# Sixteen spare products on TensorE ahead of a three-stage attention kernel's first scores

## The chip, the cores and the metric

The kernel runs on one core of one Trainium2 chip, as one program. The metric is the device time of that program in microseconds (us), as the median of several runs. Engines are named as in the profile: PE (TensorE products), PEld (TensorE weight loads), DVE (VectorE), ACT (ScalarE), POOL (GpSimd), SP (SyncE, which here issues the transfers).

## The reference

Three stages follow one another, in fp32, for 2 batches, 768 positions and 512 channels (8 heads of 64).

1. Local attention with block summaries. Each query sees the keys less than 16 positions away, and one summary for each block of 32 positions (the maximum over the block's keys, the mean over its values):

```
k_sum = k.reshape(B, H, nb, block, D).max(axis=3)
v_sum = v.reshape(B, H, nb, block, D).mean(axis=3)
scores_s = scale * einsum(q, k_sum) + log(block)
a = softmax(concat([where(|i-j| < window, scores_l, -1e9), scores_s]))
out = a @ concat([v, v_sum])
```

2. A mixture of four causal attention experts (head width 64). A gate picks two of four experts for each position; the output is the sum of the two experts' outputs with softmax weights:

```
ye = softmax(causal(scale * q @ k.T)) @ v @ wo[e]
out += mask[..., None] * w[:, :, kk:kk + 1] * ye
```

3. A mixer over positions and one over channels, each two products with a ReLU between, with residual sums:

```
u = x + (relu(x.T @ w_tok1) @ w_tok2).T
return u + relu(u @ w_ch1) @ w_ch2
```

## The kernel before

Stage 1 (`s1`, with its helpers) works for each batch through 4 head pairs of 128 partitions, and in each through 3 groups of 4 tiles of 64 queries. For a head pair, `s1_load` issues the loads on SP (L156): `kx`, the keys cut into 12 overlapping windows of 96 (for the very first pair `kt`, the plain keys, which DVE cuts up in L175 to L180), `qb`, the queries laid out as block diagonals between zeros, and `vx`, the values in windows. `s1_keys` takes the blocks' maxima on DVE (`km`, L166 or L170) and copies them behind each window (L168, L180). `s1_means` takes the blocks' means of the values with 12 small products (`vm`, L193), and POOL spreads them into `vx` (L199). `s1_scores` computes four tiles' scores into one PSUM bank (`s1s`, L205); DVE reads them with the mask (L214), ACT takes the exponentials (L217). `s1_norm` divides by the sum (DVE L223, POOL L225), `s1_turn` transposes on PE (`s1p`, L233), and `s1_values` multiplies with the values (`s1a`, L244).

Stage 2 is `proj` (the experts' projections, products `pv` and `pj`) and `attn` (`s2s` scores, `s2p` transposes, `s2a` values). Stage 3 is `tokmix` and `chmix`; `chmix` is most of the second half. The weights of stage 3 arrive as 64-bit floats and are decoded on chip by `decode_w`, which uses ACT, POOL and DVE (L126 to L136) and reads its input through a tile named `raw` with two buffers in the pool `dec`. Precise products are made of three (`mm3`, L101 to L103), on values split in a high and a low part.

What is interleaved with what is written by hand in calls of `run`. Below that, a planner lays out the order of the instructions on each engine's queue ahead of the run, from estimated times (the context is opened with `schedule_with_timeline_sim=True`, L663). Each engine then works through its queue in that order, and semaphores hold an instruction until its inputs are there. `tc.keep_in_program_order(x)` pins x behind everything traced before it on its own engine's queue; here it pins the loads of the first two head pairs.

PSUM has eight banks, given out under three tags: three for `sc`, three for `pt`, two for `acc`. The `acc` banks serve `s1a`, `s2a` and, by rotation, products of stages 2 and 3.

The change stands at the head of the traced work, directly before the loop that zeroes the four `qb` tiles (L522 to L526, on DVE at L524 and on POOL at L524 and L525).

Of the kernel before, what the change touches and what calls it, by code (L numbers as in the profile page):

```python
# [7 lines left out]
F32 = mybir.dt.float32  # L8
# [17 lines left out]
P = 128  # L26
# [16 lines left out]
def stack_kernel(ctx: ExitStack, tc, qT, kT, kwT, vw, vT, wqkv, wo, tok1, tok2, ch1, ch2,  # L43
# [5 lines left out]
    vec, act, gps, ten = nc.vector, nc.scalar, nc.gpsimd, nc.tensor  # L49
    const = ctx.enter_context(tc.tile_pool(name="const", bufs=1))  # L50
    big = ctx.enter_context(tc.tile_pool(name="big", bufs=NBIG, reuse_waits="tile"))
    dec = ctx.enter_context(tc.tile_pool(name="dec", bufs=2, reuse_waits="tile"))
# [29 lines left out]
    def bank(tag, name):  # L82
        return psa.tile([P, 512], F32, tag=tag, name=name, bufs=BK[tag])
# [431 lines left out]
    def part(gen, n):  # L515
        for _ in range(n):
            if next(gen, 1) is not None:
                return
            yield

    qbs = []
    for i in range(HP):  # L522
        qb = sp1.tile([P, ST, 2, P], F32, name="qb", bufs=2) if i < 2 else unit([P, ST, 2, P], F32, f"qb{i}")
# [150 lines left out]
```

## Time and profile before

| what | us |
|---|---|
| median of 3 runs | 471.93 (471.77 to 473.92) |
| profiled execution | 472.78 |
| its span, first to last instruction | 470.9 |
| PE busy | 445.4 (95%) |
| PE weight loads busy | 420.4 (89%) |
| POOL busy | 286.0 (61%) |
| DVE busy | 281.8 (60%) |
| ACT busy | 230.3 (49%) |
| first product on PE starts | 7.73 |
| mean granted clock of TensorE | 0.992 |

The shares are means over stages with different limits: what a change is worth has to be read in the stage where it acts. A busy PE is not PE at its peak, since ends of products are modelled. A wait is put down to the releaser that came last by the profile; where the engine named had long been done, it was another, often a transfer. The granted clock is a share of full speed: 1.00 is 2.4 GHz, 0.50 is 1.2 GHz.

### The profile page before, as it was taken

The numbers are of one execution on the slowest core, as the hardware profiler recorded it, in microseconds if no ns is written. First come the engines' busy times: TensorE is split into PE (matmuls) and PEld (weight loads), VectorE is DVE, ScalarE is ACT, GpSimd is POOL, SyncE is SP. The second block draws the span as 40 slices with busy tenths as digits, with TensorE's granted clock in tenths as the row PEclk, the third lists the DMA queues.
The fourth block names the chain that finished last, engine by engine and source line by source line (L and its number), as shares of the span: only waits on it lengthen the run. The fifth ranks groups of instructions, "written<-read, shape, count | busy, mean of one in ns | idle before, by whom it ended". The sixth has DMA issues, their size and how long they took to land.

```text
span 470.9 us, 8508 instructions
## 1 busy us (share of the span) xinstructions
PE 445.4 (95%) x3012; PEld 420.4 (89%) x3012; DVE 281.8 (60%) x817; ACT 230.3 (49%) x653; POOL 286.0 (61%) x319
## 2 busy tenths in 40 slices
PE   3998999999989969999999999999999999999996
PEld 3886999889978757888799999999999999999996
DVE  6666665749699759777864643676572673322322
ACT  2666865877778766875764333224324231110110
POOL 5674732758989877898783879877864772000000
PEclk9999999999999997999999999999999999999999
DMA  8999527706515873120211111121221110001111
GB/s 265 289 306 308 150 57 215 170 2 157 134 46 156 202 183 86 46 90 1 89 47 46 45 47 45 46 89 46 89 85 50 47 45 1 0 1 67 68 68 68
DMA packets 28522, 46.51 MB, mean 99 GB/s; under 512 B 2496, under 2 KB 19648, under 8 KB 28480
## 3 DMA queue, kind: packets, MB, share of 16 engines
q1 hardware_dynamic: 28480, 45.97, 34.7%
q8 instruction: 24, 0.39, 0.4%
q14 instruction: 18, 0.15, 0.1%
HBM read 33.38 MB, written 3.15 MB: 78 GB/s over the span
## 4 chain that ended last, share of the span: by engine, by line
PE 70%; DMA 10%; DVE 9%; POOL 5%; issue 3%; ACT 2%; SPq 0%; DVEq 0%; ACTq 0%; POOLq 0%
PE h L102 7%; PE h L103 7%; PE h L101 7%; PE o L101 7%; PE o L102 7%; PE o L103 7%; DMA kx<-in_kwT_dram 5%; PE s1s L205 3%; PE s1a L244 2%; PE u L101 2%; DMA vx<-in_vw_dram 2%; PE u L102 2%; PE u L103 2%; PE s2s L371 2%; PE s2p L397 2%
## 5 line engine op out<-in xcount | busy, mean ns | idle before, releaser
L127 POOL TENSOR_SCALAR deca<-deca 128x512 f32<-128x512 f32 x30 | 57.9, 1934 | 13.4 <-ACT deca L126 12.6
L102 PE MATMUL o<-hl,c2h 128*128 128x384 f32 x192 | 64.2, 337 | 0.0
L103 PE MATMUL o<-hh,c2l 128*128 128x384 f32 x192 | 64.0, 336 | 0.0
L97 ACT ACTIVATE hh<-h 128x384 fp32r<-128x384 f32 x48 | 23.2, 488 | 78.7 <-PE h L103 76.6
L98 DVE SCALAR_TENSOR_TENSOR hl<-h,hh 128x384 fp32r<-128x384 f32 x48 | 26.5, 555 | 53.3 <-ACT hh L97 53.3
L500 DVE TENSOR_TENSOR oa<-o,oa 128x384 f32<-128x384 f32 x64 | 31.9, 549 | 38.3 <-PE o L103 38.3
L101 PE MATMUL o<-hh,c2h 128*128 128x384 f32 x192 | 49.4, 336 | 0.0
L217 ACT ACTIVATE pr<-n,mn 128x120 f32<-128x120 f32 x96 | 36.6, 384 | 22.2 <-DVE mn L214 21.8
L133 POOL TENSOR_TENSOR raw<-raw 128x512 f32<-128x512 f32 x30 | 31.3, 1044 | 21.1 <-DVE raw L130 19.3
L387 POOL TENSOR_SCALAR pr<-pr,f,wg 128x128 f32<-128x128 f32 (+5 forms) x48 | 40.2, 850 | 4.9 <-DVE f L384 1.7
L134 POOL TENSOR_TENSOR deca<-deca,raw 128x512 f32<-128x512 f32 x30 | 40.8, 1359 | 1.0
L132 ACT ACTIVATE raw<-raw 128x512 f32<-128x512 uint32 x30 | 20.3, 677 | 36.5 <-DMA raw<-in_ch_dram 31.5
L128 DVE TENSOR_SCALAR deca<-deca 128x512 int32<-128x512 int32 x30 | 27.5, 918 | 15.2 <-POOL deca L127 15.2
L381 ACT ACTIVATE pr<-pr,mn 128x128 f32<-128x128 f32 (+5 forms) x48 | 32.1, 669 | 9.2 <-DVE mn L376 9.2
L102 PEld LDWEIGHTS o<-hl,c2h 128*128 128x128 f32 x192 | 36.0, 188 | 0.4 <-DVE hl L98 0.3
L103 PEld LDWEIGHTS o<-hh,c2l 128*128 128x128 f32 x192 | 36.0, 188 | 0.0
L205 PE MATMUL s1s<-kx,qb 128*128 128x120 f32 x192 | 28.6, 300 | 7.7 <-DVE wvl L113 7.7
L101 PEld LDWEIGHTS o<-hh,c2h 128*128 128x128 f32 x192 | 34.8, 188 | 0.1
L205 PEld LDWEIGHTS s1s<-kx,qb 128*128 128x128 f32 x192 | 26.6, 212 | 8.2 <-DVE wvl L113 7.7
L102 PE MATMUL h<-u0l,c1h 128*128 128x384 f32 x96 | 32.5, 338 | 0.0
L101 PE MATMUL h<-u0h,c1h 128*128 128x384 f32 x96 | 32.5, 338 | 0.0
L103 PE MATMUL h<-u0h,c1l 128*128 128x384 f32 x96 | 32.3, 337 | 0.0
(202 smaller groups left out, 1327.3 us busy)
## 6 DMA issues: line engine op xcount, KB each, us to landing
raw<-in_ch_dram SPq DMA_DIRECT2D x24, 512.0 KB, 3.6
kx<-in_kwT_dram SPq DMA_DIRECT2D x7, 720.0 KB, 10.2
vx<-in_vw_dram SPq DMA_DIRECT2D x8, 576.0 KB, 9.4
qb<-in_qT_dram SPq DMA_DIRECT2D x16, 192.0 KB, 8.4
raw<-in_tok_dram SPq DMA_DIRECT2D x6, 512.0 KB, 4.5
out_dram<-oa SPq DMA_DIRECT2D x16, 192.0 KB, 2.0
vt<-in_vT_dram SPq DMA_DIRECT2D x4, 384.0 KB, 10.1
rqk<-in_wqkv_dram SPq DMA_DIRECT2D x4, 256.0 KB, 10.3
```

The source lines that it names most:

```text
L101: ten.matmul(out, lh, rh, start=start, stop=False)
L102: ten.matmul(out, lh, rl, start=False, stop=False)
L103: ten.matmul(out, ll, rh, start=False, stop=stop)
L127: gps.tensor_scalar(af, af, F64_TINY, F64_HUGE, op0=ALU.max, op1=ALU.min)
L128: vec.tensor_scalar(ta, ta, 3, 0x3FFFFFFF, op0=ALU.logical_shift_left, op1=ALU.bitwise_and)
L133: gps.tensor_mul(lf, lf, ef)
L134: gps.tensor_add(af, af, lf)
L205: ten.matmul(sc[:, KX * i:KX * i + KX], qb[:, t // 2].rearrange("p i c -> p (i c)")[:, t % 2::2], kx[:, t, :], start=True, stop=True)
L217: act.activation(pr[:, i, :], n[:, i, :], AF.Exp, bias=mn[:, i:i + 1], scale=-1.0, accum_out=sm[:, i:i + 1])
L381: act.activation(prs[r], prs[r], AF.Exp, bias=mn[:, r, ci:ci + 1], scale=-1.0, accum_out=sm[:, r:r + 1])
L387: gps.tensor_scalar(prs[r][:, :nk], prs[r][:, :nk], f[:, r:r + 1], wg[:, 3 * h + r, e:e + 1], op0=ALU.mult, op1=ALU.mult)
L500: vec.tensor_add(oa[d], a[:, :HALF], oa[d])
```

## The change

Before the loop that zeroes the `qb` tiles, a tile of 128 x 128 fp32 is taken from the pool `dec` under the tag `raw`, and DVE sets it to zero. A PSUM bank is taken under the tag `acc`. PE then multiplies the zeroed tile with itself sixteen times into the same 128 columns of that bank, each product pinned behind the one before it on PE's queue. Nothing reads the bank. All else is traced as before.

```diff
+    idle = dec.tile([P, P], F32, tag="raw", name="idle")
+    vec.memset(idle, 0.0)
+    spare = bank("acc", "spare")
+    for i in range(16):
+        tc.keep_in_program_order(ten.matmul(spare[:, :P], idle, idle, start=True, stop=True))
     qbs = []
     for i in range(HP):
         qb = sp1.tile([P, ST, 2, P], F32, name="qb", bufs=2) if i < 2 else unit([P, ST, 2, P], F32, f"qb{i}")
```

## Rows read from the trace of the kernel before

**Rows 1.** The page's clock row: the span in 40 slices, in tenths.

```profile
PEclk9999999999999997999999999999999999999999
```

**Rows 2.** Chain of waits in order of time, 0 to 60 us: start, length, what.

```profile
...
7.73 9.05 DMA vx<-in_vw_dram
...
16.80 11.49 DMA kx<-in_kwT_dram
...
33.20 10.44 DMA kx<-in_kwT_dram
...
```

**Rows 3.** Windows by stage: length, engines' busy us, granted clock, DMA share, GB/s.

```profile
...
40.00:44.00 4.00, 3.07 (x38) 2.47 (x36) 2.66 (x20) 3.43 (x17) 1.18 (x2) 1.00 1.00 347
...
150.00:180.00 30.00, 23.91 (x139) 20.14 (x137) 21.26 (x58) 20.90 (x54) 23.96 (x27) 0.94 0.79 191
180.00:190.00 10.00, 9.40 (x58) 8.44 (x57) 9.39 (x28) 7.45 (x18) 7.59 (x7) 0.84 0.34 98
...
```

**Rows 4.** Timeline of PE, 0 to 24 us: start, length, instruction, count.

```profile
7.73 5.22 PE L205 MATMUL s1s<-kx,qb 128*128 128x120 f32 x24 [7.73 <-DVE wvl L113]
...
16.09 2.04 PE L205 MATMUL s1s<-kx,qb 128*128 128x120 f32 x16
...
21.02 0.69 PE L244 MATMUL s1a<-pTs,vx 120*64 120x64 f32 x16
...
```

**Rows 5.** Weight loads by shape, 7.6-12.8, 26.4-28.5, 178-183 us: busy us, mean ns.

```profile
L205 PEld LDWEIGHTS s1s<-kx,qb 128*128 128x128 f32 x24 | 5.1, 322 | 7.7 <-DVE wvl L113 7.7
...
L205 PEld LDWEIGHTS s1s<-kx,qb 128*128 128x128 f32 x16 | 2.0, 196 | 0.1
...
L371 PEld LDWEIGHTS s2s<-k,q 128*128 128x128 f32 x3 | 1.0, 331 | 0.1
...
```

**Rows 6.** Windows by stage, one of those near 178 us, columns as above.

```profile
178.00:179.00 1.00, 1.00 (x5) 0.59 (x4) 1.00 (x5) 0.00 (x0) 0.58 (x1) 0.50 0.82 184
```

**Rows 7.** Timeline of DVE, 0 to 10 us, its first three entries.

```profile
0.95 1.51 DVE L524 MEMSET qb<- 128x768 f32 x2 [0.95 <-PEq L663]
2.41 0.08 DVE L146 MEMSET kx<- 128x24 f32 x1
3.72 0.95 DVE L170 TENSOR_REDUCE km<-kt 128x24 f32<-128x768 f32 x1 [1.23 <-DMA kt<-in_kT_dram]
```

**Rows 8.** Timeline of SP, 0 to 60 us: issues of transfers.

```profile
...
1.64 0.50 SPq L540 DMA_DIRECT2D rqk<-in_wqkv_dram  x1
2.25 1.41 SPq L156 DMA_DIRECT2D qb<-in_qT_dram  x2
...
5.31 0.42 SPq L156 DMA_DIRECT2D vx<-in_vw_dram  x1
...
35.70 1.03 SPq L123 DMA_DIRECT2D raw<-in_tok_dram  x2
...
```

**Rows 9.** Instructions of tile vx, 0 to 60 us: its transfers, issue to landing.

```profile
DMA to landing us min/median/max: 5.8/9.8/12.5
```

**Rows 10.** Timeline of all engines, 13 to 50 us: waits, in brackets, for transfers and POOL.

```profile
...
17.69 1.31 POOL L112 TENSOR_SCALAR wqk0h<-rqk 128x256 fp32r<-128x256 f32 x3 [1.39 <-DMA rqk<-in_wqkv_dram]
...
18.13 1.14 DVE L113 TENSOR_TENSOR wqk0l<-rqk,wqk0h 128x256 fp32r<-128x256 f32 x2 [1.62 <-POOL wqk0h L112]
...
22.13 0.41 PEld L233 LDWEIGHTS s1p<-ident,pr 128*120 128x120 f32 x4 [0.38 <-POOL pr L225]
...
28.32 0.95 DVE L166 TENSOR_REDUCE km<-kx 128x24 f32<-128x768 f32 x1 [0.95 <-DMA kx<-in_kwT_dram]
...
43.66 0.95 DVE L166 TENSOR_REDUCE km<-kx 128x24 f32<-128x768 f32 x1 [1.34 <-DMA kx<-in_kwT_dram]
...
```

**Rows 11.** Timeline of PE, 150 to 192 us: two of its waits.

```profile
154.16 0.53 PE L371 MATMUL s2s<-k,q 128*128 128x128 f32 x2 [0.96 <-issue]
...
176.99 1.65 PE L402 MATMUL s2a<-pf,V 128*128 128x384 f32 x2 [3.87 <-ACT pf L401]
```

**Rows 12.** Timeline of ACT, 160 to 186 us: its wait for a weight transfer.

```profile
...
174.03 0.66 ACT L126 ACTIVATE deca<-raw 128x512 f32<-128x512 f32 x1 [2.61 <-DMA raw<-in_ch_dram]
...
```

## The prediction

> **What bounds the kernel now.** I read the page's clock row first, then the chain of waits in order of time, the windows by stage, and last the timeline of each engine over the first 45 us, where the change sits.
>
> The chain shows two kernels in one. Up to about 44 us it runs through three transfers one behind the other, vx from 7.73 us for 9.05, kx from 16.80 for 11.49, kx from 33.20 for 10.44 [rows 2]: 31.0 us, and PE takes part in it hardly at all. The DMA engines are still full (share 1.00) from 40 to 44 us, while PE is busy 3.07 of those 4.00 us [rows 3]. After that the chain is mostly PE's own products. So the stretch in which the change acts is bound by transfers.
>
> PE's first product starts at 7.73 us and its 24 records take 5.22 us, or 0.2175 us each; 16 records of the same line at 16.09 us take 2.04 us, 0.1275 each [rows 4]. One fp32 product is two records (24 records for the 12 products of a head pair). The reason for the two paces is seen in the weight loads: 322 ns on average at the start, 196 ns later, and 331 ns from 178 to 183 us [rows 5], where the granted clock stands at 0.50 [rows 6]. The page shows 9 for the clock from the first slice on [rows 1], but nothing ran on PE then; by the loads the engine was at the lower of its two levels, 1.2 GHz, after 7.7 idle us. From the mean, (331-322)/(331-196) = 7% of the 24 loads, one or two, were already fast: the slow stretch lasts until about 12.6 us, 4.9 us long.
>
> **The change part by part.** *The memset on DVE.* It is traced ahead of the qb memsets on the same engine. 24 columns take 0.08 us and two of 768 take 1.51 [rows 7], so 0.0009 us a column and about 0.175 us for 128; bounds 0.08 and 0.76. It moves the first qb memset's end from some 1.70 to 1.88 us. That memset releases the first qb transfer, but SP is issuing rqk until 1.64 + 0.50 = 2.14 us and the qb issue comes at 2.25 [rows 8], so 0.3 us of cover are left. The rest of DVE's queue (second qb memset, kx memset) sits in front of a wait of 1.23 us for kt [rows 7]. Cost 0; if the cover were gone, 0.1 to 0.6 us on the first load.
>
> *The sixteen products.* 32 weight loads and 32 matmul records, of 128 moving columns instead of 120. At the fast pace 0.1275 x 128/120 = 0.136 us, 4.4 us in all; at the slow one 0.232 us, 7.4 us. They start after the memset, at 0.95 + 0.175 and a semaphore, say 1.2 us. Ends: 5.6 us at the earliest, 8.6 at the latest. I take the slow stretch as before, 4.9 us: 21 records slow and 11 fast, 4.9 + 1.5 = 6.4, end at 7.6 us, against a first real product at 7.73. All of it lies in PE's idle 7.7 us. At the late bound the first scores start 0.9 us later, but then at the fast pace, and still end sooner than before.
>
> *What they give.* If the first 24 score records run fast they take 24 x 0.1275 = 3.06 us instead of 5.22: 2.16 us, of which 0.9 may be lost at the late bound and all of it if PE falls back in a gap. The bounds are thus 0 and 2.16 us, at this place.
>
> *What is late next.* PE's next work is the means, which need vx, issued at 5.31 us [rows 8]; transfers of it land 5.8 to 12.5 us after issue [rows 9], so not before 11.1 us, against the 10.8 at which PE would be ready. Then POOL stands at 17.69 us, having waited 1.39 us for rqk; DVE stands at 18.13, having waited 1.62 us for that POOL step [rows 10]. Both queues run in order, and the normalising of the next probabilities (POOL) and the reading of the next scores (DVE) stand behind these steps. Whatever arrives 2 us sooner makes these two waits longer. PE itself waits for that POOL work at 22.13 us, 0.38 us. DVE waits again for kx at 28.32 (0.95 us) and at 43.66 (1.34 us) [rows 10]. I count five places at which the lead can die, and the first already takes it: 0 reaches the end. The upper bound is the whole 2.16 us.
>
> The DMA queue: the kx transfer of 16.80 us starts as the vx ahead of it lands, 7.73 + 9.05 = 16.78 [rows 2]. Its release is a transfer and not PE, so earlier scores start it no sooner.
>
> *The tiles.* The PSUM tile takes one of the two acc banks until the last spare product; the first user of acc is at 21.02 us [rows 4]. The zeroed tile takes one of the two raw slots, whose first real load is issued at 35.70 us [rows 8]. Both are free by 8.6 us. Cost 0.
>
> The sum against the profiled execution (472.78 us, its span 470.9 and 1.9 around it): 0 + 0 + 0, bounds -2.2 and +0.6. The median of the runs shown is 471.93, 0.2% lower; I forecast against that one: 471.9.
>
> **The rivals.** *A, the lead reaches the end.* For it: PE is nearly without a gap from 7.73 to 33 us, so work it does sooner could free it for later work. Against it: the five waits above. It gives 471.9 - 2.2 = 469.7. The Trainium skill, "TensorE: Matmul & The Clock Gate" (section Terms), prices a throttled stretch at its time times one minus the clock ratio. By that rule the 4.9 us would be worth 4.9 x 0.5 = 2.45 us and the kernel would come to 469.5. The trace agrees with the size at the place (2.16 us) and speaks against carrying it to the end.
>
> *B, slower.* The order on each engine's queue is laid out ahead by a planner from estimated times, and sixteen products and a memset at the head change those estimates for PE and DVE; the order of the rest may come out anew. The sensitive place is 165 to 185 us, where decoding of the next weights and attention share ACT's in-order queue: ACT waits 2.61 us for a raw transfer [rows 12] with attention's copy behind it, PE then waits 3.87 us [rows 11], and the clock falls: 30 x 0.06 + 10 x 0.16 = 3.4 us lost by the windows [rows 3]. One such place costs 3.9 + 3.4 = 7.3 us. If a new order makes a second one, 479.2. It decides from a wait of some 2.4 us on, with the clock kept; a wait of 0.96 us cost no clock [rows 11]. For it: one late transfer was enough for this stall, and nothing pins the order at that place. Against it: the pinned products stand only at the head, and if the estimates meet again at the loads, as the trace does, the order stays.
>
> *C, faster.* The same cause with the other sign: in a new order the decode step no longer stands ahead of attention's copy, and the stall goes: 471.9 - 7.3 = 464.6; half of it gives 468.2.
>
> *D, it doesn't do what it says.* Zeros, or a gap before 7.73 us, leave PE at the lower level and the first scores keep 5.2 us. Gap and fall: PE fell after 3.87 us idle, not after 0.96 [rows 11]; the early bound of 5.6 us leaves 2.1. The time is the forecast's, 471.9.
>
> **How the numbers follow.** What a measurement of this kernel can tell from no change is about 0.5%, 2.4 us. Forecast 0.40, D 0.04: both within it. A 0.10, at 0.46% below: 0.07 within, 0.03 below. B 0.24, somewhere between 474.3 and 479.2. C 0.22, between 464.6 and 469.5. So faster 0.25, same 0.51, slower 0.24. The likeliest case's own range is 469.7 to 473 (A's gain; the memset uncovered, 0.6, and the spread of the runs shown). For 8 in 10 the range reaches into B and C until about a tenth is left out on each side: 466.5 to 478.
>
> **What the changed profile would show.** Sixteen products from about 1.2 us, weight loads of some 330 ns at first and 196 at the end; last one ended by 8.6 us. First scores in 3.1 us at 196 ns loads: the clock step right; still 322: D. Waits of POOL for rqk and of DVE for POOL before 18.13 us longer, by up to 2 us, and kx landing at the same 28.3 and 43.6 us: the step on where the lead dies right. DVE's km at 43.66 two us earlier: A. Another order of instructions on ACT, DVE or SP, and another gap of PE between 165 and 185 us: B or C, and the forecast is wrong by what that gap and its clock say.

## The result and the profile after

The changed kernel takes 473.38 us (median of 20 runs, 470.83 to 477.42) against 471.69 us for the kernel before beside it (20 runs, 468.78 to 477.0). The ratio is 1.0051, 95% interval 1.0028 to 1.0073: slower by about 2.4 us by that ratio (1.7 us between the medians), where no change was forecast. The profiled execution took 475.62 us, its span 473.8. Ratios and means further down leave out executions that were disturbed as a whole, among them the profiled ones of k3 and h3.

At the head the profile shows nearly what the change was to do. PE's timeline (start, length, instruction, count, wait in brackets), answering to [rows 4]:

```profile
1.03 5.50 PE L525 MATMUL spare<-idle 128*128 128x128 f32 x32 [1.03 <-DVE idle L522]
8.01 3.06 PE L205 MATMUL s1s<-kx,qb 128*128 128x120 f32 x24 [1.47 <-DVE wvl L113]
11.21 2.80 PE L193 MATMUL vm<-vx,blocks 96*24 96x128 f32 x24
```

and the weight loads of the first 12.8 us by shape (busy us, mean ns), answering to [rows 5]:

```profile
L525 PEld LDWEIGHTS spare<-idle 128*128 128x128 f32 x32 | 5.3, 264 | 1.0 <-DVE idle L522 1.0
L205 PEld LDWEIGHTS s1s<-kx,qb 128*128 128x128 f32 x24 | 2.9, 196 | 1.6 <-DVE wvl L113 1.6
```

The loads of the first scores went from 322 ns to 196 and their 24 records from 5.22 us to 3.06: the spare products end at 6.53 us, the higher level holds over the gap of 1.47 us, and the local gain is 2.16 us, less the 0.28 us that the scores start later. On DVE and SP, answering to [rows 7, 8]:

```profile
0.81 0.17 DVE L522 MEMSET idle<- 128x128 f32 x1 [0.81 <-PEq L668]
1.09 1.50 DVE L529 MEMSET qb<- 128x768 f32 x2
...
4.19 0.95 DVE L170 TENSOR_REDUCE km<-kt 128x24 f32<-128x768 f32 x1 [1.56 <-DMA kt<-in_kT_dram]
```

```profile
2.25 1.43 SPq L156 DMA_DIRECT2D qb<-in_qT_dram  x2
```

The qb transfer is issued at 2.25 us as before. What followed was not as before: the planner laid out another order. Over the first 55 us or so 172 places on PE, 66 on DVE, 24 on POOL, 22 on ACT and 7 on SP hold another instruction than before; behind that the order is the same to the end. The waits between 13 and 50 us, answering to [rows 10]:

```profile
26.73 1.68 POOL L112 TENSOR_SCALAR wqk1h<-rqk 128x256 fp32r<-128x256 f32 x4 [1.64 <-DMA rqk<-in_wqkv_dram]
27.17 0.60 DVE L113 TENSOR_TENSOR wqk1l<-rqk,wqk1h 128x256 fp32r<-128x256 f32 x1 [1.78 <-POOL wqk1h L112]
...
44.67 0.95 DVE L166 TENSOR_REDUCE km<-kx 128x24 f32<-128x768 f32 x1 [0.94 <-DMA kx<-in_kwT_dram]
...
48.48 0.95 DVE L186 TENSOR_REDUCE vs<-vt 128x24 f32<-128x768 f32 x1 [1.21 <-DMA vt<-in_vT_dram]
```

Set beside the same product of before, PE is 1.7 us ahead at 12 us, 2.4 to 3.5 ahead at 38 to 42, and 0.8 behind at 50. Part of that is the new order's own: run e2 further down, the same order without the products, is 0.8 to 2.2 us ahead of before at 38 to 42. Against e2 the products' lead is 1.6 us at 12 and 38 us, 1.2 at 42, and gone at 44: it ends at a landing of kx. PE then falls 4 us further behind between 84 and 90 us. There the second batch's first loads (kx, qb, vt, vx) and the queries and keys of stage 2 (q, k) are moved in one burst; between 74 and 91 us the DMA share is 1.00 in both kernels. The kernel before, all engines, 76 to 91 us:

```profile
77.44 0.55 SPq L156 DMA_DIRECT2D vt<-in_vT_dram  x1
...
80.71 0.95 DVE L166 TENSOR_REDUCE km<-kx 128x24 f32<-128x768 f32 x1 [2.70 <-DMA kx<-in_kwT_dram]
...
83.55 0.95 DVE L186 TENSOR_REDUCE vs<-vt 128x24 f32<-128x768 f32 x1 [0.81 <-DMA vt<-in_vT_dram]
...
85.50 2.21 PE L205 MATMUL s1s<-kx,qb 128*128 128x120 f32 x16
```

and the changed kernel there:

```profile
78.00 0.55 SPq L156 DMA_DIRECT2D vt<-in_vT_dram  x1
...
81.94 0.95 DVE L166 TENSOR_REDUCE km<-kx 128x24 f32<-128x768 f32 x1 [3.35 <-DMA kx<-in_kwT_dram]
...
87.36 0.95 DVE L186 TENSOR_REDUCE vs<-vt 128x24 f32<-128x768 f32 x1 [3.39 <-DMA vt<-in_vT_dram]
...
89.17 3.22 PE L205 MATMUL s1s<-kx,qb 128*128 128x120 f32 x16 [2.38 <-DVE mn L214]
```

DVE starts the sums of vt (vs) 5.42 us after km instead of 2.84, since vt lands late. The reading of the scores stands behind vs in DVE's queue, so PE waits 2.38 us, where before it waited for nothing, and its sixteen records then take 3.22 us instead of 2.21: the granted clock falls. The windows (length, busy us of PE, PEld, DVE, ACT, POOL, then clock, DMA share, GB/s) of before and after:

```profile
76.00:96.00 20.00, 19.98 (x210) 17.77 (x208) 12.04 (x70) 15.78 (x67) 11.90 (x30) 1.00 0.77 198
```

```profile
76.00:96.00 20.00, 17.58 (x156) 15.74 (x154) 10.28 (x62) 11.37 (x48) 8.86 (x23) 0.91 0.82 206
```

PE idles 2.42 of 20 us instead of 0.02 and loses 20 x 0.09 = 1.8 us to the clock. The stall near 177 us [rows 11] is smaller in this execution, which gives part of that back: PE's line after, and the same line in another execution of the kernel before (run f1):

```profile
179.33 0.91 PE L402 MATMUL s2a<-pf,V 128*128 128x384 f32 x2 [1.32 <-ACT pf L401]
```

```profile
176.67 0.91 PE L402 MATMUL s2a<-pf,V 128*128 128x384 f32 x2 [1.67 <-ACT pf L401]
```

The same kernel before waits 3.87 us in one execution and 1.67 in another, without a fall of the clock (1.00 over that whole execution). So that stall belongs to an execution. Whether the one at 85 us does too is a question for many profiles.

### The profile page after: what moved, and what is told of

It reads as the page before. It is cut to its first block, busy times and chain, and to the rows that moved or that the text cites. A ratio compares the mean times of both kernels' runs of the same rounds, so it can differ in the third digit from the quotient of the medians.

```text
span 473.8 us, 8573 instructions
## 1 busy us (share of the span) xinstructions
PE 449.8 (95%) x3044; PEld 422.8 (89%) x3044; DVE 283.2 (60%) x818; ACT 231.5 (49%) x653; POOL 286.6 (61%) x319
## 5 line engine op out<-in xcount | busy, mean ns | idle before, releaser
L101 PE MATMUL h<-u1h,c1h 128*128 128x384 f32 x96 | 32.3, 336 | 0.0
L102 PE MATMUL h<-u1l,c1h 128*128 128x384 f32 x96 | 32.3, 336 | 0.0
```

What stands on the lines that cost most here:

```text
L101: ten.matmul(out, lh, rh, start=start, stop=False)
L102: ten.matmul(out, lh, rl, start=False, stop=False)
```

## The experiments

Each run was timed in five rounds beside the kernel before; intervals are 95%. Where a kernel is said to keep the order of before, the first 55 us of all five queues are pinned to it:

```diff
+    order = {
+        "DVE": (1, [0, 1, 2, 3, 4, 5, 7, 8, 9, 10, 11, 6, 33,
...
+    for e, (skip, seq) in order.items():
+        for x, y in zip(seq, seq[1:]):
+            tc.add_manual_dep(traced[e][skip + y], traced[e][skip + x].name,
...
```

**Is it the new order?** Run e1 is the change with the order of before; e2 the new order without the products; e3 the change with SP's seven transfers back in place; e4 the kernel before with SP's new order alone.

> The sixteen products and the memset as in the change, but every queue (PE, DVE, ACT, POOL, SP) pinned to the order of the kernel before over its first 55 us, the stretch in which the two orders differ. Theory O (the new order of the queues costs the time, the products nothing): first scores in 3.1 us instead of 5.2, the lead dead by 45 us, SP issuing raw at about 35.7 us as before; ratio to before 0.996 to 1.002. Theory P (the products themselves cost it: their place on PE, the moved phase of the clock, the longer program): 1.003 to 1.007, as the change.

> No products and no memset, but every queue pinned to the order that the changed kernel has. Theory O: the cost comes without the products, ratio 1.003 to 1.010 (the first scores also run slow again, 5.2 us, so perhaps a little more than the change's 1.005); PE waits for ACT at about 50 us for 1.5 us or more, as after. Theory P: 0.998 to 1.002.

> The change, but seven transfers on SP between 33 and 42 us (vt, vt, raw, raw, qb, qb, vx) pinned to the order of before; the other queues keep the order of after but for 2 places on DVE, 2 on ACT and 12 on PE, between 45 and 60 us. Theory S (within O, the transfers' order is what costs: the key sums on DVE at 48.5 us wait 1.2 us for a vt issued later): the wait is gone, ratio to before 0.997 to 1.002. Theory O without S (the order on PE and DVE): 1.003 to 1.007. Theory P: 1.003 to 1.007.

> The kernel before with nothing changed but the order of the same seven transfers on SP, pinned to that of after (qb, qb, vt, vx, vt, raw, raw). Theory S: DVE waits for vt at about 48 us and PE for 1.5 to 2 us behind it; ratio 1.002 to 1.006. Theory O without S and theory P: 0.998 to 1.002.

Measured: e1 1.0037 (0.9998 to 1.0077), e2 0.9993 (0.9958 to 1.0028), e3 1.0009 (0.9973 to 1.0046), e4 1.0020 (0.9986 to 1.0054). The intervals overlap, so three kernels ran again, with the kernel before as a fourth to see what chance alone does.

> The kernel before, unchanged, as a control beside the shared runs of the kernel before: every theory gives 0.997 to 1.003. Its second profile shows what of the first one belongs to the kernel and what to one run: theory N (the stages from 80 us on differ from run to run, by waits for transfers and falls of the clock, as much as the change differs from before) expects the fall of the clock at 177 us, or its wait of 3.9 us, to be gone or of another size, with the same order of instructions.

> The change, unchanged. Theories O and P: ratio 1.003 to 1.007 again, and the waits of 3.4 us for vt at 87 us with the fall of the clock behind it in this profile too. Theory N: 0.999 to 1.005, and the wait at 87 us smaller and without a fall of the clock; the wait of PE at 50 us (1.6 us) stays, since it follows from the order.

> Products with the old order, as e1, now beside the change itself. Theory P: as high as the change within 0.2%. Theory O: 0.997 to 1.001, below the change by 0.3% or more. Theory N: all four kernels of this batch within 0.4% of each other.

> The new order without products, as e2, beside the change itself. Theory P: 0.998 to 1.002, below the change by 0.3% or more. Theory O: as high as the change within 0.2%. Theory N: within 0.4% of the others.

Measured: f1 0.9997 (0.9964 to 1.0030), the change 1.0050 (1.0014 to 1.0086), products in the old order 1.0022 (0.9987 to 1.0058), the new order without products 0.9998 (0.9967 to 1.0030). The new order alone shows no cost, twice. Theory O, which expected one, fell; what costs goes with the products. Single timings hold a ratio to about 0.35% either way, and e3, which has the products, came at 1.0009.

**What in the products?** Four of them (g1); sixteen with 16 moving columns (g2); thirty-two (g3, h3); sixteen on two zeroed tiles and two banks, so that all later tiles of those tags fall into the slots of before (g4). The order is that of before in all (g1 keeps it unpinned, but for two memsets on POOL).

```diff
-    for i in range(16):
+    for i in range(4):
```

```diff
-        tc.keep_in_program_order(ten.matmul(spare[:, :P], idle, idle, start=True, stop=True))
+        tc.keep_in_program_order(ten.matmul(spare[:, :16], idle, idle[:, :16], start=True, stop=True))
```

```diff
-    for i in range(16):
+    for i in range(32):
```

```diff
+    idle2 = dec.tile([P, P], F32, tag="raw", name="idle")
+    vec.memset(idle2, 0.0)
+    spare2 = bank("acc", "spare")
...
+        tc.keep_in_program_order(ten.matmul((spare, spare2)[i % 2][:, :P], (idle, idle2)[i % 2], (idle, idle2)[i % 2], start=True, stop=True))
```

> The change with 4 products instead of 16. The queues keep the order of before by themselves (two memsets on POOL change places). PE falls idle from about 2.8 to 7.7 us, so the first scores run slow again, 5.2 us. Theory W (the cost follows from PE being fast and ahead before the data): 0.998 to 1.002. Theory D (each product costs, wherever it comes from): a quarter of the cost of 16, 1.000 to 1.002. Theory T (the two tiles cost, not the products: raw and acc buffers change places in all that follows): as the change, 1.003 to 1.005. Theory N (no cost, spread of runs): 0.997 to 1.003.

> Sixteen products of 16 columns instead of 128 with the order of before pinned: same instructions, an eighth of the columns. Ended by about 5 us. Theory W: 0.998 to 1.002 if the first scores are slow again (5.2 us), 1.002 to 1.005 if they are fast (3.1 us). Theory D: 1.002 to 1.005. Theory T: 1.003 to 1.005. Theory N: 0.997 to 1.003.

> Thirty-two products with the order of before pinned. They end at about 10.9 us (32 more records at 0.136 us than the change's 6.5), so the first scores start 3.2 us later and end at about 14 us instead of 12.9. Forecast's step (transfers bind up to 44 us, so even this start is absorbed by the waits for rqk and kx): the same time as with 16 and the old order, 1.000 to 1.005. Theory D: twice the cost of 16, 1.004 to 1.008. Theory T: 1.003 to 1.005.

> Sixteen products with the order of before pinned, but on two zeroed tiles and two banks in turn, so that the raw and acc buffers of all later work fall as in the kernel before. Theory T: 0.998 to 1.002. Theories W and D: 1.002 to 1.005, as e1 and f3. Theory N: 0.997 to 1.003.

Measured: g1 0.9991 (0.9947 to 1.0034), g2 1.0038 (1.0000 to 1.0075), g3 1.0070 (1.0036 to 1.0105), g4 1.0038 (1.0001 to 1.0075). The slots are not it: g4 has those of before and is no faster. Nor is the early rise of the clock: in g2 PE's weight loads stay slow through the products and into the first scores, and the ratio is no lower. That four cost nothing is less sure, since g1's interval would also hide a quarter of the cost of sixteen (theory D).

```profile
L525 PEld LDWEIGHTS spare<-idle 128*128 128x128 f32 x32 | 6.9, 332 | 1.0 <-DVE idle L522 1.0
L205 PEld LDWEIGHTS s1s<-kx,qb 128*128 128x128 f32 x24 | 4.8, 306 | 0.0
```

**Is it the time, or the reading?** Thirty-two products of 16 x 16 results (h1), thirty-two that read one partition (h2), the thirty-two full ones again (h3). A new theory, R: the products' reading of 128 partitions beside the first loads makes these land later.

```diff
-        tc.keep_in_program_order(ten.matmul(spare[:, :P], idle, idle, start=True, stop=True))
+        tc.keep_in_program_order(ten.matmul(spare[:16, :16], idle[:, :16], idle[:, :16], start=True, stop=True))
```

```diff
-        tc.keep_in_program_order(ten.matmul(spare[:, :P], idle, idle, start=True, stop=True))
+        tc.keep_in_program_order(ten.matmul(spare[:, :P], idle[:1, :], idle[:1, :], start=True, stop=True))
```

> Thirty-two products of 16 x 16 instead of 128 x 128, order of before pinned: as many instructions as g3, an eighth of the weights and of the columns read from SBUF. They should end before 7.7 us, so the first scores are not held up. Theory I (the cost goes with the number of instructions): 1.005 to 1.009, as g3. Theory R (it goes with what PE reads of SBUF and how long, while the first loads are written): 0.999 to 1.003. Theory N (no cost, the ratios so far are spread): 0.997 to 1.003.

> Thirty-two products of 128 x 128 that read one partition only, order of before pinned: number and length as g3, what is read of SBUF a 128th. First scores from about 10 us as in g3. Theory R: 0.999 to 1.003, and the first qb not late. Theory I: 1.005 to 1.009. Theory L (the late first scores themselves cost in g3): as g3, 1.004 to 1.009, with h1 near 1.000.

> g3 once more, beside h1 and h2 on the same chip: theories I, R and L 1.004 to 1.009; theory N 0.997 to 1.003.

Measured: h1 0.9991 (0.9957 to 1.0026), h2 1.0057 (1.0032 to 1.0082), h3 1.0016 (0.9980 to 1.0051). The 64 small records take 1.89 us and show no cost. g3 and h3 are one kernel; the mean of their ratios is 1.0043, and h3 alone fell below what theories I, R and L said of it. The one-partition ones take far longer than the full ones and hold up the first scores; PE's timeline of h2:

```profile
1.03 14.02 PE L525 MATMUL spare<-idle 1*128 1x128 f32 x64 [1.03 <-DVE idle L522]
14.98 5.26 PE L205 MATMUL s1s<-kx,qb 128*128 128x120 f32 x23
```

Its cost is thus that of a start 7.3 us late (14.98 against 7.73), of which 0.0057 x 472 = 2.7 us arrive; that the late start is the reason is not shown apart. It does not judge R; sixteen such products, which end at 8.2 us, do:

> The change with sixteen products that read one partition of the zeroed tile instead of 128 (same moving columns, same number of records, order of the kernel before kept). They should last some 6.9 us at the lower clock (32 x 0.215), about as long as the full ones, while drawing 1/128 of the bytes. Theory R (full products' reading beside the first loads makes these land later): ratio to the kernel before 0.998 to 1.001, POOL's first conversion of rv at 5.3 to 5.45 us and first scores at 7.6 to 7.75 us. Rival (PE being occupied to the end of its idle time is what costs, whatever it reads): ratio 1.002 to 1.005.

> Sixteen full products in the order of the kernel before, beside the two one-partition runs on the same chip. So far 1.0037, 1.0022. Theory R: 1.002 to 1.005 and above the one-partition runs by 0.2 to 0.4%; first conversion of rv at 5.4 to 5.8 us. If the cost seen so far were chance: 0.999 to 1.001.

> The same kernel as k1 a second time, since one timing of five rounds holds the ratio only to about 0.35% either way. Theory R 0.998 to 1.001, rival 1.002 to 1.005; a mean of the two runs above 1.0025 drops R.

Measured: one partition 1.0025 (0.9990 to 1.0059) and 1.0077 (1.0037 to 1.0118), full ones 1.0063 (1.0032 to 1.0094). The mean of the two is 1.0051, above the 1.0025 that was to drop R: R fell too. In k2's profile the first loads even land on time (scores at 7.76 us), and the kernel is slower all the same. The rival that stood beside R, that PE being occupied to the end of its idle time is what costs, gave 1.002 to 1.005; it fits these timings.

**What is left: the number of instructions, or the time that they take.** Ten timings of sixteen products, wide, narrow or of one partition, in either order, have a mean ratio of 1.0041; four, or thirty-two tiny ones, 0.9991 each. What all the sixteens share is 32 weight loads and 32 matmul records more at the head of PE's queue, and also 5.5 to 7.2 us of work there; the four and the tiny ones take 2.07 and 1.89 us. An engine's instructions are themselves fetched over the DMA engines; the trace has those packets as kind "instruction". On queue q8 there are 24 of 16 KB over the span, and they shift with the number of PE's instructions, so I take them as reads of PE's code. One of them lies in the burst at 76 to 90 us. The rows by queue (packets, MB, share) where it falls: the kernel before from 84 to 86 us; k2 from 78 to 80; the changed kernel from 80.5 to 82.5; h1 from 74.5 to 76.

```profile
q8 instruction: 1, 0.02, 4.2%
```

```profile
q8 instruction: 1, 0.02, 2.8%
```

```profile
q1 hardware_dynamic: 706, 0.65, 102.5%
q8 instruction: 1, 0.02, 2.8%
```

```profile
q8 instruction: 1, 0.02, 3.9%
```

Before, it starts at 84.2 us, when vt has landed (vs starts at 83.55). With sixteen products it starts ahead of km, in the middle of the transfers of kx, qb and vt; one packet takes 0.9 to 1.5 us. Over 18 profiles, with the fetch's start and the start of vs given against that of km, and idle time of PE as 20 us less its busy time in the window 76 to 96 us:

| products at the head | profiles | fetch against km, us | km to vs, us (mean) | PE idle, us (mean) |
|---|---|---|---|---|
| none or 4 | 6 | +2.4 to +3.6 | 2.84 to 4.19 (3.23) | 0 to 1.17 (0.27) |
| 16, any kind | 9 | -1.7 to -0.4 | 3.71 to 5.42 (4.37) | 0.69 to 2.42 (1.30) |
| 32 | 3 | -6.1 to -5.3 | 2.84 to 3.62 (3.25) | 0.03 to 0.62 (0.29) |

k2, timeline of 76 to 91 us and window:

```profile
80.01 0.95 DVE L166 TENSOR_REDUCE km<-kx 128x24 f32<-128x768 f32 x1 [2.64 <-DMA kx<-in_kwT_dram]
...
84.28 0.95 DVE L186 TENSOR_REDUCE vs<-vt 128x24 f32<-128x768 f32 x1 [2.25 <-DMA vt<-in_vT_dram]
...
86.10 2.34 PE L205 MATMUL s1s<-kx,qb 128*128 128x120 f32 x16 [1.17 <-DVE mn L214]
```

```profile
76.00:96.00 20.00, 18.81 (x188) 16.57 (x186) 11.90 (x69) 14.55 (x64) 10.84 (x28) 1.00 0.72 191
```

and with four products (g1), window alone:

```profile
76.00:96.00 20.00, 19.95 (x194) 17.61 (x193) 12.36 (x71) 15.05 (x65) 11.02 (x28) 1.00 0.79 211
```

Sixteen products cost 1.30 - 0.27 = 1.03 us of idle PE here, and in two of nine profiles the wait also pulled the clock down to 0.91 over the window (1.8 us each, 0.4 on average): 1.4 us together. The ten timings say 0.0041 x 472 = 1.9 us. With 32 the fetch falls ahead of these transfers, into those of q, of which four are issued before kx. The transfers of q, issue to landing, in the kernel before and in h1, g3 and h2:

```profile
DMA to landing us min/median/max: 2.7/3.3/3.7
```

```profile
DMA to landing us min/median/max: 2.6/4.3/4.4
```

```profile
DMA to landing us min/median/max: 2.6/4.2/5.1
```

```profile
DMA to landing us min/median/max: 2.6/4.4/5.4
```

In the fifteen profiles with fewer products the longest takes 3.5 to 3.7 us. So a second group of transfers is late when a fetch falls into it, and here no wait of PE follows (0.03 to 0.62 us idle). That the full thirty-twos and those of one partition pay for their late start instead is not shown.

How far this is shown: that the cost comes with the products, and not with the new order, the slots, the early clock or the reading, is shown by the timings. They do not tell the number of products from the time that they take. The profiles do, at this burst: the place of the fetch goes with the number, be the products long or short, and in g3 and h2, where they last 9 and 14 us, vt is not late. That vt takes longer with sixteen products (7.8 us from issue to landing on average, 6.7 without), and that PE idles for it, is shown too. That the fetch is what delays vt fits all three rows and the transfers of q, but no run moved a fetch alone; and one execution of the kernel before (f1) has 4.19 us from km to vs with the fetch behind km, so there may be another cause of late vt.

That this delay is the whole 1.9 us is not shown. The nine profiles with sixteen products reach the burst sooner than the six with none or four (vt issued at 77.6 us on average against 78.7), so vt lands at the same 85.4 us in both, and the nine executions took 472.4 us on average against 472.1. What they lose at the burst is measured against their own lead there, and their totals do not contain the cost that the timings show. Nor is the clock the missing part: by the mean granted clock on record for every execution, 115 with sixteen products lose 1.9 us each to it, and 179 of the kernel before or of its new order alone lose 1.6.

## Why the prediction was wrong

**What bounds the kernel** was right for the first 44 us, which is where I looked. The second burst of transfers, at 74 to 91 us with a DMA share of 1.00, was not in the argument, and the waits of PE that came with the products stand there.

**The memset** took 0.17 us (0.175 said) and hid behind SP's other issues. Right.

**The sixteen products** took 5.50 us (6.4 said, bounds 4.4 to 7.4): by (331-264)/(331-196) = 50% of their loads were fast, 16 of 32 instead of the 11 assumed. The trace's first record of the granted clock, 1.00, starts at 4.54 us in the changed kernel and at 12.55 us in the kernel before; the page counts what lies ahead of the first record as full, which is why its clock row [rows 1] shows 9 from the start. **What they give** was right to the hundredth: 3.06 us. Rival D is out.

**What is late next** was right: the lead goes into waits for transfers. It shows plainly with the order of before, in k2, whose first scores start at 7.76 us. PE's first means and DVE's first km from a loaded kx, in the kernel before and in k2 (there also POOL's step on rqk):

```profile
12.87 2.80 PE L193 MATMUL vm<-vx,blocks 96*24 96x128 f32 x24
...
12.88 0.95 DVE L166 TENSOR_REDUCE km<-kx 128x24 f32<-128x768 f32 x1 [0.38 <-DMA kx<-in_kwT_dram]
```

```profile
11.18 2.80 PE L193 MATMUL vm<-vx,blocks 96*24 96x128 f32 x24 [0.35 <-DMA vx<-in_vw_dram]
...
12.84 0.95 DVE L166 TENSOR_REDUCE km<-kx 128x24 f32<-128x768 f32 x1 [1.43 <-DMA kx<-in_kwT_dram]
...
17.61 1.31 POOL L112 TENSOR_SCALAR wqk0h<-rqk 128x256 fp32r<-128x256 f32 x3 [1.34 <-DMA rqk<-in_wqkv_dram]
```

DVE has lost the lead at the landing of kx, POOL's step on rqk starts at 17.61 us instead of 17.69 [rows 10], and PE's lead of 1.7 us at the means is 0.1 at 28 us. The first of the five waits, for vx, took only 0.35 us of it; the wait that takes it, for this kx, was not among the five. In the changed kernel, with its new order, the lead lasts to the landing of kx near 44 us. Rival A is out. The Trainium skill, "TensorE: Matmul & The Clock Gate" (section Terms), prices a throttled stretch at its time times one minus the clock ratio. By that price the stretch was worth 2.45 us, an estimate; the trace has 2.16 us of it at the place, and none of the ten timings has any at the end.

**The tiles** show no cost: g4, with all slots as before, is no faster.

**The step that failed** is "All of it lies in PE's idle 7.7 us", by which the products became a 0 in the sum 0 + 0 + 0. They were costed by their time alone. Their time is hidden, and the kernel is slower all the same: by 1.9 us on average over ten timings of sixteen products, 2.4 in the first, against an upper bound of 0.6 that came only from the memset. What the runs show in its place is a price of the products that their place in idle time does not take away, with 1.0 us more idle PE behind a late vt at 76 to 96 us as the one place where it is seen. That it comes from their 64 instructions, behind which all of PE's code is fetched at another moment, is the likeliest reason and not proven; the rest of the cost stays open.

**Rival B** had the right sign and the wrong cause. The order did come out anew, at the head only, and shows no cost (e2, f4). Its price of 7.3 us, and that of C, was read from a stall of 3.87 us that another execution of the same kernel does not have (1.67 us, clock kept): one profiled execution was taken for the kernel.

## What to carry to other kernels

Work put into an engine's idle time can cost more than its time. One place to look is where the engine's code fetches lie against a burst of transfers, above all where DMA is full and something waits. A lead won ahead of transfer-bound work ended here at a later landing, however clean the local gain. Before a price is taken from a stall in one profile, see whether a second profile of the same kernel has it, and before a loss found in profiles is called the cause, see whether their totals contain it.

## What was not expected of the hardware

Two kinds of product at the head left PE's weight loads at the slow pace although it worked without a gap: 16 moving columns (7.0 us, loads 332 ns in g2) and one partition (13.7 us of loads, 327 ns in h2; 6.9 us, 327 ns in k1). Behind sixteen full ones the loads take 196 ns. PE's code (as I take queue q8 to be) comes in 24 reads of 16 KB, each 0.9 to 1.5 us long beside full transfers. And two executions of one kernel differ in a single wait (3.87 against 1.67 us) by about as much as the whole change is worth, so its 0.5% needed 20 runs, while five-round timings of the same kernel came out at 1.0025 and 1.0077.
